# Weight sums mostly on GpSimd in a new order, the features' sum over tokens by fp32 column tiles, state products of two tiles together

## The chip, the cores and the metric

The kernel runs on one core of a Trainium2 chip. The metric is device time in microseconds (us) of one execution. A core has a matrix engine (PE; its weight loads are listed apart as PEld), three engines for elementwise work (DVE, the vector engine; ACT, the scalar engine; POOL, GpSimd), the queue engine SP that only starts DMAs, and DMA engines that move data between HBM and the on-chip memory SBUF. PSUM is the memory that the matrix engine writes to: eight banks of 128 x 512 fp32.

## The reference, cut to what matters

```python
S, D, H, Dh, F = 2048, 512, 32, 16, 1376
xn = layernorm(x)                                  # x: 2048 x 512
q, k, v = split_heads(xn @ wqkv)                   # 32 heads of 16
pq, pk = q @ w_phi, k @ w_phi                      # per head, 16 x 16
phi = concat(softmax(p), softmax(-p))              # for pq and pk: 32 features a head
kv = sum over tokens of phi_k^T v                  # per head 32 x 16
z  = sum over tokens of phi_k                      # per head 32
o  = (phi_q @ kv) / (phi_q . z + 1e-6)
s  = merge_heads(o) @ wo
h  = relu(xn @ W_gate) * (xn @ W_up)               # 2048 x 1376
out = x + s * silu(h @ W_down)
```

`z` is what the first line of the title calls the features' sum over tokens; `kv` is the state.

## The kernel before, in words

All products are done in a split form: a number is written as a high part (`h`) and a low part (`l`) that TensorE's fast fp32r mode takes, and `mm3` issues three matmuls (low x high, high x low, high x high) for each 128 rows of the inner dimension. Every instruction goes through a recorder (`InOrder`, line 60 of the profile), so all profile rows have the line L60 and are told apart by names.

**First part, tokens.** The 2048 tokens are 16 tiles of 128, `n` = 0..15. After two tiles by themselves, the loop `pair(m)`, m = 1..7, takes tiles n = 2m and n + 1 together. Each tile gets keys `pk`, values `pv`, queries `pq` (these go out to DRAM for later), the exponentials `ek` of the keys' features with their sums `sm` and reciprocals `rc`, and the product `ek * rc` = phi (`features_k`). `features_split` then starts a DMA from POOL's queue that adds phi to the buffer `zacc` (`zacc<-ek`; each waits in POOL's queue until the one before has landed, because both write `zacc`), and `kv_products` adds phi^T v of the tile to the PSUM bank `PKV`, in 16 small matmuls in four column tiles of 32.

From pair 3 on (`seven`, `FIRST = 3`) the key and value products of a pair use seven block products instead of eight. This needs sums of weight blocks, made once in pairs 1 to 3: `T[0]` to `T[3]`, each with two halves k = 0, 1 and a high and low part. The table `PLAN` says at which named point of which pair each step is issued, and on which engine: `vc20` is "on DVE (`v`), combine (`c`), sum 2, half 0"; `g` is POOL; `h` is the high part, always on ACT (`sh00`); `l` the low part. `T[0]` is needed first in pair 3 (the `pv` block), then `T[1]` and `T[2]` in the `pk` blocks, and `T[3]` (`th`) in the second half of the pair.

In pair 3 and later PE's order is: 6 matmuls `pk` (A11), 6 `pv` with `T[0]`, 6 `pk` with `T[1]`, 6 `pk` (A12), 6 `pk` with `T[2]`, [`kv_products(n - 2)`], transposes `pxT` of a coming tile, 12 `pq`, `kv_products(n - 1)`, 6 `pk` with `T[3]`, 6 `pv`, transposes, 12 `pq`. The same sums of columns are made of the tokens: POOL's `xf`, then `XT<-sb` and `XT<-xf`, which the `pv` block with `T[0]` of the next pair reads.

`MULT` names the engine of the product `ek * rc`: POOL for even tiles, DVE (None) for odd ones.

**Second part, the wide layer.** For f = 0..10 (128 of the 1376 columns, padded, each) `gate_up` does seven blocks of 6 matmuls (`pa`, `pb`, `pc`, `pd`), for each half of the tokens; `down` and `out_tile` follow (`py`, `pso`). In the first half `f_prep(f)` makes the weight sums of f: 6 copies on ACT, about ten operations on POOL (`tab`, `wa`, `wb`, `wc`, `wd`, `fdl`), and nine DMAs that spill the result to DRAM (`ws`), from which `f_reload` brings it back for the second half. f = 0 and 1 are prepared in pair 7, f in the block before it. At the same time `state()` turns the key state, and `q_pair` treats the saved queries; its GpSimd step `weigh` needs `zB`, the sum z.

**The sum z before.** When the last `zacc` DMA has landed, ACT copies the high part `zh`, POOL makes the low part `zl`, and four matmuls 128 x 512 (`pz`) with a matrix of ones sum over the partitions, which are tokens; ACT copies the diagonal pieces to `zB` in eight instructions. One matmul with `noughts` writes zeros to the upper half of `PKV` in pair 1.

**What sets the order.** `Clock` keeps a modelled time for each engine while the program is written. Background work is a list of generators; `pump()` advances each whose condition holds by the model. The order of each engine is fixed when the kernel is built. Nothing is reordered on the chip, apart from weight loads.

Of the kernel before, what the change touches and what calls it, by code (L numbers as in the profile page):

```python
# [10 lines left out]
ALU = mybir.AluOpType  # L11
# [21 lines left out]
UNITS = [*(((0, j), (1, j)) for j in range(2)), ((2, 0), (2, 1)),  # L33
         *(((q, j), (q + 1, j)) for q in (6, 4) for j in range(2)), ((3, 0), (3, 1))]
LAST = [2 * q + j for q in QUERIES[1] for j in range(2)][-3:]
AHEAD = ()
FIRST = 3
PLAN = {(1, "sums"): "vc50 vc51", (1, "split a"): "gc00", (1, "end"): "gc01", (2, "start"): "vc10", (2, "split b"): "vc11 vc20 gc21", (2, "scaled"): "gc30", (2, "mid"): "sh20 sh21 gl20 sh00 sh01 sh11", (2, "split a"): "vl11", (2, "turned"): "vl00 vl01 vc31", (2, "end"): "sh10 gl10 gc40", (3, "start"): "gl21 gc41 sh30", (3, "split b"): "gl30", (3, "sums"): "sh31", (3, "mid"): "vl31"}

START = (14, 15)  # L40
WO_WITH = (4, 5, 6, 7)
# [119 lines left out]
def layer_kernel(ctx: ExitStack, tc: tile.TileContext, x, wkT, wqT, wv, wo, wf, cst, out):  # L161
# [30 lines left out]
    def mm(o, w, m, start, stop):  # L192
        nc.tensor.matmul(o, w, m, start=start, stop=stop, skip_group_check=True)
# [288 lines left out]
    def kv_products(n):  # L482

        phi, v = PHI.pop(n).rearrange("p (j a c) s f -> p c j a (s f)", a=2, c=4), VH.pop(n)
        v = v.rearrange("p (c j x) -> p c j x", c=4, j=4)
        if n == 0:
            PKV.append(ps((P, 8, 64), name="pkv"))
        for j in range(4):
            for c in range(4):
                r = slice(32 * c, 32 * c + 32)  # L490
                nc.tensor.matmul(PKV[0][r, j], v[:, c, j], phi[:, c, j], start=n == 0 and j == 0,
                                 stop=n == N - 1, skip_group_check=True, tile_position=(0, 32 * c))
        if n == 0:
            mm(PKV[0].rearrange("p j x -> p (j x)")[:, 256:], noughts[:, :P], noughts, False, False)


    RAW, FT, WD = {}, {}, {}
# [7 lines left out]
    DONE = set()  # L505

    def f_load(f):
        if f in AHEAD[-1:]:

            t = u4((P, 2, 2, 2, P), "rawg")  # L510
            RAW[f] = [t[:, c] for c in range(2)], u2((P, D), "rawd")
            nc.sync.dma_start(t.rearrange("p c k s f -> p (c k s f)"), wf[f][:, :1024])
        else:
            RAW[f] = two("rawg", f not in AHEAD), u2((P, D), "rawd")
            for c in range(2):
                nc.sync.dma_start(RAW[f][0][c].rearrange("p k s f -> p (k s f)"), wf[f][:, c * 512:(c + 1) * 512])
        nc.sync.dma_start(RAW[f][1], wf[f][:, 1024:])

    def w_pair(name):
# [10 lines left out]
    def f_prep(f, keep=True):  # L530


        rg, rd = RAW.pop(f)
        b11, b12, b21, b22 = (rg[c][:, :, s, :] for c in range(2) for s in range(2))
        ta, tb = two("tab", keep)
        yield "gpsimd", b22
        add(nc.gpsimd, tb[:, 0], b12, b11, ALU.subtract)
        add(nc.gpsimd, ta[:, 1], b22, b12, ALU.subtract)
        wa = w_pair("wa")
        yield "scalar", b11  # L540
        for c in range(2):
            nc.scalar.activation(wa[0][:, c], rg[c][:, :, 0, :], AF.Copy)
        put(f, 0, wa[0])
        yield "gpsimd", ta
        add(nc.gpsimd, ta[:, 0], b22, tb[:, 0], ALU.subtract)
        add(nc.gpsimd, tb[:, 1], b21, ta[:, 0], ALU.subtract)
        wb = w_pair("wb")
# [24 lines left out]
        yield from sums_of(fd[1], rd, f32(fd[0]), ALU.subtract, fd[0])  # L572
        put(f, 8, fd[1])
        if keep:
            FT[f], WD[f] = [wa, wb, wc, wd], fd
            nxt = f + 1
            while nxt in AHEAD:
                nxt += 1
            del rg, rd, ta, tb
            if nxt < NF:  # L580
                f_load(nxt)
        DONE.add(f)
        yield None,
# [412 lines left out]
    noughts = u2((P, 256), "noughts", F32R)  # L996
    nc.vector.memset(f32(noughts), 0.0)
    zacc = u4((P, H, 2, DH), "zacc")

    WK, WV, WQ = w_tile("wk"), w_tile("wv"), w_tile("wq")  # L1000
# [115 lines left out]

    def all_preps():
        for f in AHEAD:
            f_load(f)
            yield 30,  # L1120
            yield from f_prep(f, False)
        while at[0] < START[0] - 1:
            yield 3,
        f_load(0)
        yield 30,
        for f in range(NF):
            if f not in AHEAD:
# [47 lines left out]
    def pair(m):  # L1175
# [48 lines left out]
        if news:  # L1224
            norm_scale(*news)
        t_steps(m, "scaled")
        kv_products(n - 2)
        pace.pump()
        at[0] = n + 1
        if n + 3 < N:  # L1230
# [46 lines left out]
        t_steps(m, "end")  # L1277
        pace.pump()

    EB, MULT = [], [nc.gpsimd, None]  # L1280
    for m in range(1, NP):
        pair(m)
    features_k(N - 1, *EB.pop())
# [2 lines left out]

    kvacc, zB = [None] * 2

    one, ones = u2((P, P), "one"), u2((P, P), "ones", F32R)
    nc.vector.memset(one, 1.0)  # L1290
    nc.scalar.activation(ones, one, AF.Copy)
    zhl = [u4((P, 1024), f"z{s}", F32R) for s in "hl"]
    kvt = sb.tile([P, NG, 32], F32, tag="kvt", bufs=1, name="kvt")
    nc.vector.memset(kvt, 0.0)
    q_load(0)
# [4 lines left out]
    def state():  # L1300
        nonlocal kvacc, zB
        kv_products(N - 1)

        kvacc = u2((P, 256), "kvacc")
        nc.scalar.activation(kvacc, PKV[0][:, :4].rearrange("p j x -> p (j x)"), AF.Copy)
        yield "vector", kvacc
        kvT = u2((P, 256), "kvT")
        nc.vector.transpose(kvT, kvacc)
        kvT = kvT.rearrange("p (j x f) -> p j x f", x=4, f=DH)
        kvacc = None  # L1310
        for c in range(4):
            r, h = slice(32 * c, 32 * c + 32), c % 2
            nc.vector.tensor_copy(kvt[r, :, DH * h:DH * h + DH].rearrange("p (j a) f -> p j a f", a=2), kvT[r, :, 0:4:3, :])
        zB = small(256, "zB", 1).rearrange("p (d x) -> p d x", d=4)
        while zhl[1].name not in pace.ready:
            yield 1,
        for a in range(2):
            yield "tensor", zhl[1]
            p = ps((P, 4, 4, 32), name="pz")
            for i, z in enumerate(zhl[::-1]):  # L1320
                mm(p.rearrange("p d i x -> p (d i x)"), ones, z[:, a * 512:(a + 1) * 512], i == 0, i == 1)
            for i in range(4):
                r = slice(32 * i, 32 * i + 32)
                nc.scalar.activation(zB[r, :, 32 * a:32 * a + 32], p[r, :, i, :], AF.Copy)

    def z_parts():
        yield "scalar", zacc
        nc.scalar.activation(zhl[0], flat(zacc), AF.Copy)
        yield "gpsimd", zhl[0]
        add(nc.gpsimd, zhl[1], flat(zacc), f32(zhl[0]), ALU.subtract)  # L1330
        yield None,

    def all_queries(half):
        if not half:
            pace.add(z_parts(), first=True)
# [161 lines left out]
```

## Time and profile before

| what | value |
|---|---|
| three runs | 564.0, 561.24, 562.82 us; median 562.82 us |
| the profiled execution's own time | 562.98 us |
| its span on the core | 561.2 us |
| PE busy | 548.0 us of the span (98%), 3149 matmuls |
| POOL busy | 347.9 us (62%) |
| DVE busy | 383.3 us (68%) |
| ACT busy | 263.6 us (47%) |
| mean granted TensorE clock | 0.991 |
| DMA moved | 125.45 MB, mean 224 GB/s |

The profiled execution took 562.98 us; 1.8 us of it lie around the span. How to read a row of a timeline: start in us, duration, engine, operation, output <- inputs, shapes, count; a bracket gives idle time of the engine before it and what ended it. Matmul rows overlap: in a full stream a 128 x 512 matmul starts every 0.227 us (six in 1.36 us), though each is shown with 0.39 us. fp32 matmuls count twice in the rows ("x32" for 16). "PEclk" is the clock that the chip granted TensorE, 1.00 for full speed.

### The profile page before, as it was taken

Reading aid. Unit: us, or ns where it says so; the run is one execution under the profiler, and the core shown is the slowest. Engines: PE = TensorE matmul, PEld = TensorE weight load, DVE = VectorE, ACT = ScalarE, POOL = GpSimd, SP = SyncE. Lnnn points to the kernel's source line nnn. Section 1 sums busy time; section 2 is a strip of 40 time slices with the busy share of each in tenths; the row PEclk is TensorE's granted clock in tenths of the full one; section 3 lists DMA queues with packets and bytes.
Section 4 is the critical chain, followed back from the end, with each engine's and each line's share of the span. In section 5 each row is a group of like instructions: output and inputs, shape, how many; then the busy total and the mean of one; then the engine's idle time right before and its main releaser. Section 6 shows DMA issues by size and latency. Waiting matters only on the chain.

```text
span 561.2 us, 9072 instructions
## 1 busy us (share of the span) xinstructions
PE 548.0 (98%) x3149; PEld 444.8 (79%) x3149; DVE 383.3 (68%) x588; ACT 263.6 (47%) x467; POOL 347.9 (62%) x309
## 2 busy tenths in 40 slices
PE   9999979999997999999999999999999999999997
PEld 8888758777775886887878888888778787878886
DVE  5998678867654669698953442599999496743323
ACT  3886656654542565646453142223564535342510
POOL 1566855542974999899996316352556584843491
PEclk9999979999999999999999999999999999999999
DMA  8359655646698767867697999594674462848063
GB/s 287 130 163 307 191 130 160 165 109 152 186 291 273 256 241 256 299 224 282 243 313 280 340 425 404 181 385 146 207 243 133 163 212 87 288 134 316 1 225 113
DMA packets 76223, 125.45 MB, mean 224 GB/s; under 512 B 6673, under 2 KB 29073, under 8 KB 75281
## 3 DMA queue, kind: packets, MB, share of 16 engines
q1 hardware_dynamic: 73872, 116.94, 59.7%
q0 software_dynamic: 2160, 7.87, 7.1%
q8 instruction: 25, 0.41, 0.3%
q14 instruction: 22, 0.17, 0.1%
q10 hardware_dynamic: 144, 0.07, 0.0%
HBM read 67.96 MB, written 48.50 MB: 208 GB/s over the span
## 4 chain that ended last, share of the span: by engine, by line
PE 77%; POOL 8%; DVE 5%; DMA 5%; issue 4%; ACT 0%; SPq 0%; POOLq 0%; DVEq 0%; ACTq 0%
PE py L60 18%; PE pk L60 9%; PE pd L60 8%; PE pa L60 8%; PE pso L60 8%; PE pq L60 7%; PE pb L60 7%; PE pc L60 4%; PE pv L60 4%; DMA zacc<-ek 2%; DMA wvr<-wv 2%; PE pkv L60 2%; POOL tab L60 1%; PE pnum L60 1%; POOL ez L60 1%
## 5 line engine op out<-in xcount | busy, mean ns | idle before, releaser
L60 PE MATMUL py<-fdh,hl 128*128 128x512 f32 x176 | 69.0, 392 | 0.0
L60 PE MATMUL py<-fdl,hh 128*128 128x512 f32 x176 | 68.5, 389 | 0.0
L60 PE MATMUL py<-fdh,hh 128*128 128x512 f32 x176 | 68.5, 389 | 0.0
L60 PE MATMUL pa<-XT,wa 128*128 128x512 f32 x264 | 67.3, 390 | 0.0
L60 PEld LDWEIGHTS pa<-XT,wa 128*128 128x128 f32 x264 | 49.4, 188 | 10.7 <-issue 0.4
L60 DVE TENSOR_TENSOR y<-py,y 128x512 f32<-128x512 f32 x40 | 27.5, 689 | 35.5 <-PE py L60 35.5
L60 POOL TENSOR_TENSOR hl<-t,hh 128x512 fp32r<-128x512 f32 x16 | 20.7, 1295 | 40.7 <-ACT hh L60 40.3
L60 POOL TENSOR_TENSOR y<-y,ys 128x512 f32<-128x512 f32 x24 | 30.9, 1292 | 17.4 <-ACT ys L60 17.1
L60 PE MATMUL pq<-XT,wqh 128*128 128x512 f32 (+1 forms) x144 | 40.5, 367 | 0.0
L60 PEld LDWEIGHTS py<-fdh,hl 128*128 128x128 f32 x176 | 33.0, 188 | 8.5 <-issue 1.2
L60 PEld LDWEIGHTS py<-fdh,hh 128*128 128x128 f32 x176 | 33.0, 188 | 6.9
L60 POOL TENSOR_TENSOR ez<-eq,zB 128x1024 f32<-128x1024 f32 x16 | 38.4, 2411 | 0.1
L60 PEld LDWEIGHTS py<-fdl,hh 128*128 128x128 f32 x176 | 33.0, 188 | 6.7
L60 ACT ACTIVATE hh<-t 128x512 fp32r<-128x512 f32 x16 | 10.1, 632 | 56.3 <-DVE t L60 53.0
L60 PE MATMUL pd<-XT,wd 128*128 128x512 f32 x132 | 34.2, 393 | 1.2 <-DVE t L60 1.2
L60 PE MATMUL pb<-XT,wb 128*128 128x512 f32 x132 | 34.3, 396 | 0.0
L60 PE MATMUL pd<-XT,wc 128*128 128x512 f32 x132 | 33.9, 391 | 0.0
L60 PE MATMUL pc<-XT,wb 128*128 128x512 f32 x132 | 33.5, 389 | 0.0
L60 DVE TENSOR_REDUCE mx<-pk 128x32 f32<-128x512 f32 x32 | 20.6, 684 | 18.8 <-PE pk L60 18.8
L60 POOL TENSOR_TENSOR ol<-of,oh 128x512 fp32r<-128x512 f32 (+1 forms) x13 | 19.8, 1550 | 20.3 <-ACT oh L60 20.3
L60 PE MATMUL pk<-wkh,XT 128*128 128x512 f32 x88 | 31.1, 405 | 0.0
L60 PEld LDWEIGHTS pd<-XT,wd 128*128 128x128 f32 x132 | 24.5, 188 | 7.7 <-POOL wd L60 1.6
(194 smaller groups left out, 1440.5 us busy)
## 6 DMA issues: line engine op xcount, KB each, us to landing
zacc<-ek POOLq DMA_DIRECT2D x15, 512.0 KB, 5.3
xts<-XT SPq DMA_DIRECT2D x4, 1792.0 KB
XT<-xts SPq DMA_DIRECT2D x7, 1024.0 KB, 6.7
rawg<-wf SPq DMA_DIRECT2D x22, 256.0 KB, 3.1
ws<-wa SPq DMA_DIRECT2D x22, 256.0 KB, 4.5
ws<-wb SPq DMA_DIRECT2D x22, 256.0 KB, 4.8
ws<-wc SPq DMA_DIRECT2D x22, 256.0 KB, 5.0
wa<-ws SPq DMA_DIRECT2D x22, 256.0 KB, 5.4
```

Source lines behind the costliest of these rows:

```text
L60: return self.tc.keep_in_program_order(op(*a, **k))
```

## The change

1. `PLAN`: most combine and low-part steps go to POOL (15 steps with `g`, 5 with `v`; before, 10 and 10), in a new order. The first ones come earlier in pairs 1 and 2.
2. `MULT`: both tiles' products `ek * rc` on POOL in the pair loop.
3. `kv_products(n - 2)` is issued right before `kv_products(n - 1)`, half a pair later than before.
4. z: the chain `zh`, `zl`, `pz` goes. Four fp32 matmuls with one column of 32 ones as weights, one for each column tile, read `zacc` itself and write to the upper half of `PKV`; one ACT copy makes `zB`. The `noughts` matmul goes.
5. `AHEAD`: f = 2 is loaded and prepared in pairs 4 to 6 (from tile 9 on), in large buffers, is spilled, and read back in the block of f = 1.

```diff
-AHEAD = ()
+AHEAD, AT = (2,), (9,)
 FIRST = 3
-PLAN = {(1, "sums"): "vc50 vc51", (1, "split a"): "gc00", (1, "end"): "gc01", (2, "start"): "vc10", (2, "split b"): "vc11 vc20 gc21", (2, "scaled"): "gc30", (2, "mid"): "sh20 sh21 gl20 sh00 sh01 sh11", (2, "split a"): "vl11", (2, "turned"): "vl00 vl01 vc31", (2, "end"): "sh10 gl10 gc40", (3, "start"): "gl21 gc41 sh30", (3, "split b"): "gl30", (3, "sums"): "sh31", (3, "mid"): "vl31"}
+PLAN = {(1, "sums"): "gc51", (1, "mid"): "gc50", (1, "split a"): "vc01 gc11", (1, "turned"): "gc00", (1, "end"): "gc10", (2, "start"): "vc21", (2, "sums"): "sh00 gc20", (2, "scaled"): "sh20 sh01 gl00", (2, "split a"): "sh21 gl20 gl01", (2, "turned"): "sh10 sh11 vc31 gl10", (2, "end"): "gl21", (3, "start"): "gc30 vl11 gc40 vc41", (3, "sums"): "sh30 sh31 gl30 gl31"}
...
-        if n == 0:
-            mm(PKV[0].rearrange("p j x -> p (j x)")[:, 256:], noughts[:, :P], noughts, False, False)
...
-        if f in AHEAD[-1:]:
-            t = u4((P, 2, 2, 2, P), "rawg")
-            RAW[f] = [t[:, c] for c in range(2)], u2((P, D), "rawd")
+        if f in AHEAD:
+            t = u8((P, 2, 2, 2, 2, P), "rawg")
+            RAW[f] = [t[:, 0, c] for c in range(2)], u2((P, D), "rawd"), [t[:, 1, c] for c in range(2)]
...
-        wa = w_pair("wa")
+        if keep:
+            wa, wb = w_pair("wa"), None
+        else:
+            t = u8((P, 4, 2, 2, P), "wab", F32R)
+            wa, wb = (t[:, 0], t[:, 1]), (t[:, 2], t[:, 3])
...
         for f in AHEAD:
+            while at[0] < AT[AHEAD.index(f)]:
+                yield 3,
             f_load(f)
             yield 30,
             yield from f_prep(f, False)
...
         t_steps(m, "scaled")
-        kv_products(n - 2)
         pace.pump()
...
         t_steps(m, "split a")
+        kv_products(n - 2)
         kv_products(n - 1)
...
-    EB, MULT = [], [nc.gpsimd, None]
+    EB, MULT = [], [nc.gpsimd, nc.gpsimd]
...
-    one, ones = u2((P, P), "one"), u2((P, P), "ones", F32R)
-    nc.vector.memset(one, 1.0)
-    nc.scalar.activation(ones, one, AF.Copy)
-    zhl = [u4((P, 1024), f"z{s}", F32R) for s in "hl"]
+    ones = small(32, "ones", 1)
+    nc.vector.memset(ones, 1.0)
...
+        yield "tensor", zacc
+        z = flat(zacc).rearrange("p (a d i x) -> p i a d x", a=2, d=4, i=4)
+        for i in range(4):
+            r = slice(32 * i, 32 * i + 32)
+            nc.tensor.matmul(PKV[0][r, 4:].rearrange("p (a b) (d x) -> p a (b d) x", a=2, x=32), ones, z[:, i], start=False,
+                             stop=True, skip_group_check=True, tile_position=(0, 32 * i))
         zB = small(256, "zB", 1).rearrange("p (d x) -> p d x", d=4)
-        while zhl[1].name not in pace.ready:
-            yield 1,
-        for a in range(2):
-            yield "tensor", zhl[1]
-            p = ps((P, 4, 4, 32), name="pz")
-            for i, z in enumerate(zhl[::-1]):
-                mm(p.rearrange("p d i x -> p (d i x)"), ones, z[:, a * 512:(a + 1) * 512], i == 0, i == 1)
-            for i in range(4):
-                r = slice(32 * i, 32 * i + 32)
-                nc.scalar.activation(zB[r, :, 32 * a:32 * a + 32], p[r, :, i, :], AF.Copy)
...
+        nc.scalar.activation(zB.rearrange("p d (a x) -> p a d x", a=2),
+                             PKV[0][:, 4:].rearrange("p (a b) (d x) -> p a (b d) x", a=2, x=32), AF.Copy)
```

**Place 1, POOL from the end of pair 2 into pair 3, before.** `l_854` and `l_855` are the low parts of `T[2]`, `l_865` that of the first half of `T[1]`, `t_815` and `t_816` lead to `T[3]`; the first `zacc` is that of tile 4.

```order
L60 TENSOR_TENSOR XT<-xf,XT 128x2x2x128
L60 DMA zacc<-ek 128x1024
L60 TENSOR_TENSOR l_865<-wvr,h_863 128x512
L60 TENSOR_TENSOR t_815<-t_815,wkl 128x512
L60 TENSOR_TENSOR l_855<-t_463,h_853 128x512
L60 TENSOR_TENSOR t_816<-t_816,wkl 128x512
L60 DMA zacc<-ek 128x1024
L60 TENSOR_TENSOR th<-t_815,th 128x512
```

The same place after the change: `l_818` and `l_819` are the low parts of `T[2]`, `l_810` that of the second half of `T[0]`, `l_953` that of the first half of `T[1]`, `t_957` leads to `T[3]`, and `ek` is the product of tile 5, which DVE did before.

```order
L60 TENSOR_TENSOR XT<-xf,XT 128x2x2x128
L60 DMA zacc<-ek 128x1024
L60 TENSOR_TENSOR l_818<-t_460,h_816 128x512
L60 TENSOR_TENSOR l_810<-wvr,h_809 128x512
L60 TENSOR_TENSOR l_953<-wvr,h_951 128x512
L60 TENSOR_TENSOR l_819<-t_461,h_817 128x512
L60 TENSOR_TENSOR ek<-ek,rc 128x1024
L60 TENSOR_TENSOR t_957<-wkh,wvr 128x512
L60 TENSOR_TENSOR t_957<-t_957,wkl 128x512
L60 DMA zacc<-ek 128x1024
```

Between the two `zacc` stand seven operations where there were four. Two of them, `l_810` and `l_953`, are read by PE in the first blocks of pair 3.

**Place 2, DVE at the same time, before:** `l_860` is the low part of `T[0]`.

```order
L60 TENSOR_TENSOR ek<-mx,pk 128x32x16
L60 TENSOR_TENSOR l_860<-wvr,h_859 128x512 x2
L60 TENSOR_TENSOR t_816<-wkh,wvr 128x512
L60 TENSOR_TENSOR XT<-pxT,XT 128x2x2x128
L60 TENSOR_REDUCE sm<-ek 128x64
L60 RECIPROCAL pk<-sm 128x64
L60 TENSOR_TENSOR ek<-ek,pk 128x1024
```

And after: `l_954` is the low part of the second half of `T[1]`; before the change it stood, as `l_866`, five instructions ahead of `l_860`.

```order
L60 TENSOR_TENSOR ek<-mx,pk 128x32x16
L60 TENSOR_TENSOR t_958<-wkh,wvr 128x512
L60 TENSOR_TENSOR XT<-pxT,XT 128x2x2x128
L60 TENSOR_REDUCE sm<-ek 128x64
L60 RECIPROCAL rc<-sm 128x64
L60 TENSOR_TENSOR l_954<-wvr,h_952 128x512
L60 TENSOR_TENSOR t_958<-t_958,wkl 128x512
```

The `T[0]` steps are gone from DVE; two steps with `t_958` and `l_954` stand there now, behind the sums of tile 5.

**Place 3, PE at the start of the second part, before,** from the state product of tile 15 to the matmuls of z:

```order
L60 MATMUL pkv<-ek,v 32x64 x16
L60 MATMUL pd<-XT,wc 128x512 x3
L60 MATMUL pc<-XT,wc 128x512 x6
L60 MATMUL pa<-XT,wa 128x512 x6
L60 MATMUL pd<-XT,wd 128x512 x6
L60 MATMUL pa<-XT,wa 128x512 x6
L60 MATMUL pz<-zl,ones 128x512
L60 MATMUL pz<-zh,ones 128x512
```

And after:

```order
L60 MATMUL pkv<-ek,v 32x64 x16
L60 MATMUL pd<-XT,wc 128x512 x3
L60 MATMUL pkv<-zacc,ones 32x256 x4
L60 MATMUL pc<-XT,wc 128x512 x6
L60 MATMUL pa<-XT,wa 128x512 x6
L60 MATMUL pd<-XT,wd 128x512 x6
L60 MATMUL pa<-XT,wa 128x512 x6
```

The matmuls of z stand 24 matmuls earlier in PE's order than before.

More of the change, by code (lines that the diff above doesn't have):

```diff
@@ L507, in f_load @@
     def f_load(f):
-        if f in AHEAD[-1:]:
-            t = u4((P, 2, 2, 2, P), "rawg")
-            RAW[f] = [t[:, c] for c in range(2)], u2((P, D), "rawd")
-            nc.sync.dma_start(t.rearrange("p c k s f -> p (c k s f)"), wf[f][:, :1024])
-        else:
-            RAW[f] = two("rawg", f not in AHEAD), u2((P, D), "rawd")
-            for c in range(2):
-                nc.sync.dma_start(RAW[f][0][c].rearrange("p k s f -> p (k s f)"), wf[f][:, c * 512:(c + 1) * 512])
+        if f in AHEAD:
+            t = u8((P, 2, 2, 2, 2, P), "rawg")
+            RAW[f] = [t[:, 0, c] for c in range(2)], u2((P, D), "rawd"), [t[:, 1, c] for c in range(2)]
+        else:
+            RAW[f] = two("rawg", True), u2((P, D), "rawd"), None
+        for c in range(2):
+            nc.sync.dma_start(RAW[f][0][c].rearrange("p k s f -> p (k s f)"), wf[f][:, c * 512:(c + 1) * 512])
         nc.sync.dma_start(RAW[f][1], wf[f][:, 1024:])
@@ L530, in f_prep @@
     def f_prep(f, keep=True):
-        rg, rd = RAW.pop(f)
+        rg, rd, tab = RAW.pop(f)
         b11, b12, b21, b22 = (rg[c][:, :, s, :] for c in range(2) for s in range(2))
-        ta, tb = two("tab", keep)
+        ta, tb = tab or two("tab", True)
         yield "gpsimd", b22
@@ L546, in f_prep @@
         add(nc.gpsimd, tb[:, 1], b21, ta[:, 0], ALU.subtract)
-        wb = w_pair("wb")
+        wb = wb or w_pair("wb")
         yield "scalar", ta
@@ L578, in f_prep @@
                 nxt += 1
-            del rg, rd, ta, tb
+            del rg, rd, ta, tb, tab
             if nxt < NF:
@@ L995, in layer_kernel @@
     nc.vector.memset(mhalf, -0.5)
-    noughts = u2((P, 256), "noughts", F32R)
-    nc.vector.memset(f32(noughts), 0.0)
     zacc = u4((P, H, 2, DH), "zacc")
@@ L1313, in state @@
             nc.vector.tensor_copy(kvt[r, :, DH * h:DH * h + DH].rearrange("p (j a) f -> p j a f", a=2), kvT[r, :, 0:4:3, :])
-        zB = small(256, "zB", 1).rearrange("p (d x) -> p d x", d=4)
-        while zhl[1].name not in pace.ready:
-            yield 1,
-        for a in range(2):
-            yield "tensor", zhl[1]
-            p = ps((P, 4, 4, 32), name="pz")
-            for i, z in enumerate(zhl[::-1]):
-                mm(p.rearrange("p d i x -> p (d i x)"), ones, z[:, a * 512:(a + 1) * 512], i == 0, i == 1)
-            for i in range(4):
-                r = slice(32 * i, 32 * i + 32)
-                nc.scalar.activation(zB[r, :, 32 * a:32 * a + 32], p[r, :, i, :], AF.Copy)
[L1326 to L1331, printed above, removed]
+        yield "tensor", zacc
[4 more added lines that the diff above has]
+                             stop=True, skip_group_check=True, tile_position=(0, 32 * i))
+        zB = small(256, "zB", 1).rearrange("p (d x) -> p d x", d=4)
+        nc.scalar.activation(zB.rearrange("p d (a x) -> p a d x", a=2),
+                             PKV[0][:, 4:].rearrange("p (a b) (d x) -> p a (b d) x", a=2, x=32), AF.Copy)
     def all_queries(half):
         if not half:
-            pace.add(z_parts(), first=True)
             yield from state()
```

## The prediction, made before the changed kernel had run

> **What bounds the kernel now.** I read the page's busy times first, then the waits of PE, then PE's timeline where it waits.
>
> ```profile
> PE 548.0 (98%) x3149; PEld 444.8 (79%) x3149; DVE 383.3 (68%) x588; ACT 263.6 (47%) x467; POOL 347.9 (62%) x309
> ...
> PE pz L60 <- POOL zl L60: 3.4, 1, 3.4
> PE pv L60 <- DVE l L60: 2.5, 1, 2.5
> PE pd L60 <- DVE t L60: 1.2, 1, 1.2
> ...
> PE pk L60 <- ACT pk L60: 1.0, 1, 1.0
> ...
> 70.00:84.00 14.00, 10.40 (x62) 7.36 (x62) 11.00 (x18) 6.85 (x14) 7.10 (x6) 0.76 0.56 134
> ```
>
> PE sets the time: 548.0 of 561.2 us busy. Work taken from another engine is worth something only where PE waits for it, and that is in few places. The two large ones are the places that the change touches. The window from 70 to 84 us (the column after POOL's is the granted clock) shows that a wait costs more than itself: at a mean clock of 0.76, 14 us lose 3.4 us of full speed.
>
> The first hole is the start of pair 3:
>
> ```profile
> 68.46 0.39 PE L60 MATMUL pk<-wkh,XT 128*128 128x512 f32 x1
> ...
> 72.74 0.47 PE L60 MATMUL pv<-l,XT 128*128 128x512 f32 x1 [2.53 <-DVE l L60]
> ...
> 75.12 0.79 PE L60 MATMUL pk<-h,XT 128*128 128x512 f32 x1 [0.98 <-ACT pk L60]
> ...
> 82.68 0.65 PE L60 MATMUL pkv<-ek,v 128*32 128x64 f32 x32
> ```
>
> Between 68.46 and 82.68 stand 30 matmuls, which in a full stream take 30 x 0.227 = 6.8 us. They took 14.2, so this hole costs **7.4 us**: idle time, and then half clock. The second hole is the sum z:
>
> ```profile
> 171.59 1.53 PE L60 MATMUL pc<-XT,wc 128*128 128x512 f32 x6
> ...
> 175.68 1.52 PE L60 MATMUL pa<-XT,wa 128*128 128x512 f32 x6
> 180.63 0.80 PE L60 MATMUL pz<-zl,ones 128*128 128x512 f32 x1 [3.43 <-POOL zl L60]
> ...
> 184.58 1.54 PE L60 MATMUL pc<-XT,wb 128*128 128x512 f32 x6
> ```
>
> After `pa` (175.68 + 1.36 = 177.04; six matmuls take 6 x 0.227 = 1.36) only the 6 matmuls of `pb` would stand before 184.58 without z: 178.4. This hole costs **6.2 us**, `pz` itself included.
>
> **Change 1, the sums' steps.** What makes DVE late before is in POOL's and DVE's timelines around 65 us, and, for a second case, near 212 us (the two short rows are from the chain of waits):
>
> ```profile
> 57.92 0.87 POOL L60 DMA_DIRECT2D zacc<-ek  x1 [5.73 <-DVE XT L60]
> 58.53 1.59 POOL L60 TENSOR_TENSOR wvr<-wvr 128x512 f32<-128x512 f32 x1
> 59.79 1.00 POOL L60 TENSOR_TENSOR lr<-lr,mhalf 128x2 f32<-128x2 f32 x1
> ...
> 61.74 1.69 POOL L60 TENSOR_TENSOR xf<-xf,sb 128x256 f32<-128x256 f32 x2
> ...
> 64.38 2.17 POOL L60 TENSOR_TENSOR ek<-ek,rc 128x1024 f32<-128x1024 f32 x1
> 66.28 1.53 POOL L60 TENSOR_TENSOR XT<-sb,XT 128x512 fp32r<-128x512 f32 x1
> 67.52 1.53 POOL L60 TENSOR_TENSOR XT<-xf,XT 128x512 fp32r<-128x512 f32 x1
> ...
> 64.70 4.91 DVE L60 TENSOR_TENSOR l<-wvr,h 128x512 fp32r<-128x512 f32 x1 [3.54 <-POOL l L60]
> ...
> 74.33 1.20 DVE L60 TENSOR_REDUCE sm<-ek 128x64 f32<-128x1024 f32 x1
> 75.56 0.56 DVE L60 RECIPROCAL pk<-sm 128x64 f32<-128x64 f32 x1
> ...
> 211.84 1.80 DVE L60 SCALAR_TENSOR_TENSOR qd<-qs 128x64 f32<-128x64 f32 x1
> ...
> 211.61 1.25 POOL hl L60
> 212.86 0.70 POOL tab L60
> ```
>
> The DVE operation at 64.70, with both inputs in SBUF, took 4.91 us. It ended at 69.61, some 0.6 us after POOL's run of `ek`, `XT`, `XT` (to 69.05). So it did not get in at POOL's boundaries at 66.3 and 67.5. The small one at 211.84 sat through `hl` and `tab` in the same way and ended at 213.64, just after POOL's 213.56, where POOL's next operation had to wait for its own predecessor. My reading: such a DVE operation waits until POOL has a gap.
>
> The Trainium skill says (SBUF — State Buffer, "Who interferes with whom") that a DVE instruction with two SBUF inputs contends with a GpSimd one that reads SBUF, and that the second to issue is blocked until the first finishes. The trace agrees on the contention; the 4.91 us span three POOL instructions, where the page speaks of one. By the page's rule the first rival below would come true.
>
> Now the walk with the new order. Before the change `zacc` of tile 3 starts at 57.92; I keep that. Spacings come from the starts above: 1.25 for 512 columns, 0.7 `lr`, 1.4 `xf`, 1.9 `ek`, 0.6 to 0.7 for issuing a DMA. POOL then does one combine (59.8), `lr` (60.5), `l` of `T[0]`'s first half (61.7), `xf` (63.1), `ek` (65.0), two `XT` (67.5), `zacc` of tile 4 (68.2), and without a gap `l_818` (69.4), `l_810` (70.7), `l_953` (71.9), `l_819` (73.2), `ek` of tile 5 (75.1), `t_957` (76.3). The next `t_957` depends on it: a gap. DVE comes to `t_958`, two SBUF inputs, after its `ek` pieces, near 65, and gets in during the `zacc` issue, to 68.2. Then `XT` 0.6, `sm` 1.2, `rc` 0.55: it asks for `l_954` at 70.6, inside POOL's run, and finishes it at **77.0**.
>
> PE reaches pair 3 about 0.6 us earlier than before (change 2), so its `T[0]` block starts at 69.2. It needs the second half's `l_810` at 70.1: 0.6 late. It needs `l_953` at 71.4: 0.5 late. It needs `l_954` at 72.8: 4.2 late. That is 5.3 us idle, and after such an idle time I put the same loss of clock as before, 3.4 us: 8.7 against 7.4. **+1.3 us** (bounds: -0.4 where half the clock loss is spared, +3 where DVE gets in only behind the `zacc` of tile 5). The moved steps themselves, some five of 1.25 us from DVE to POOL, cost nothing else: no later wait of PE names them.
>
> Both `ek` on POOL (14 us more, 7 x 1.9) and f = 2's preparation (ten operations, about 9.6 us by the ones of f = 0) lie in pairs 3 to 7. They must not delay the sums for the next pair's `pv`:
>
> ```profile
> 119.59 0.57 POOL L60 TENSOR_TENSOR lr<-lr,mhalf 128x1 f32<-128x1 f32 x1 [3.17 <-DVE lr L60]
> ...
> 126.00 1.30 POOL L60 TENSOR_TENSOR XT<-xf,XT 128x512 fp32r<-128x512 f32 x1
> ...
> 129.71 1.36 PE pv L60 x6
> ```
>
> In pair 5 `XT` ends at 127.3, 2.4 us before `pv`. Of the new work only `wc` (1.3) falls between `xf` and `XT`, and 0.6 of ACT's new copies ahead of `vb`; the rest falls where POOL idles (3.17 here). 0.5 us is left: cost 0. Where that cover fails, each us late is a us of PE.
>
> **Change 2, state products together.**
>
> ```profile
> 54.85 0.39 PE L60 MATMUL pv<-wvh,XT 128*128 128x512 f32 x1
> 55.17 0.65 PE L60 MATMUL pkv<-ek,v 128*32 128x64 f32 x32
> ...
> 65.02 0.40 PE L60 MATMUL pv<-wvh,XT 128*128 128x512 f32 x1
> 65.26 0.60 PE L60 MATMUL pxT<-ident,xt 128*128 128x128 f32 x4
> ```
>
> With 16 products between, `pxT` starts at 55.75 (the row after 55.17), 0.90 after the last `pv`; without, 0.24. One group alone costs 0.66. Behind another group it costs at most its own 0.58 (55.17 to 55.75), and at least 0.45 if its turn-around goes too. That saves 0.08 to 0.21 in each of 7 pairs, plus 0.2 for the `noughts` matmul: 0.8 to 1.7, I take **-1.1**. Phi of the odd tile now comes from POOL; it is needed half a pair later, after 12 `pq`.
>
> **Change 3, the sum z.** PE comes to z 24 matmuls earlier. Its input is the landed `zacc`:
>
> ```profile
> 161.08 0.88 POOL L60 DMA_DIRECT2D zacc<-ek  x1 [2.56 <-DMA zacc<-ek]
> ...
> 166.94 10.07 DMA zacc<-ek
> ...
> 177.10 1.06 ACT L60 ACTIVATE zh<-zacc 128x1024 fp32r<-128x1024 f32 x1 [5.79 <-DMA zacc<-ek]
> ...
> DMA to landing us min/median/max: 2.9/5.2/10.1
> ```
>
> The last DMA landed at 177.0, and PE stands at z at 171.6. It waits 5.4 us, does four matmuls of 256 columns (as many columns as one state group, 0.58; twice that at half clock: 1.1), and then runs at half clock for some 4 us, as it did from 180.63 to 184.58, which loses 1.8. That is 8.3 against 6.2: **+2.1**. The chain `zh`, `zl` and nine ACT copies saved do not help, since PE now waits for the DMA itself. With a landing in 5.2 us the wait would be 0.5 and the step worth -5.0; I take the row of this very DMA, since the same spills and loads of f = 0 and 1 run beside it. What z feeds (`weigh`) comes some tens of us later.
>
> **Change 5, the wide layer.** POOL is freed of f = 2's work; PE waits there once, 1.2 us for `t`. Bounds -1.2 to 0; I take 0, since that wait hangs on DVE's queue. Nine reads of 256 KB come into the block of f = 1, ahead of their use.
>
> **Sum.** 1.3 - 1.1 + 2.1 + 0 = +2.3 on the profiled 562.98 us (0.16 above the median): **565.3 us**.
>
> **Rival 1: DVE gets in between POOL's instructions.** Then `l_954` follows `l_810`: 71.3, in time for 72.8. Pair 3 loses 1.1 instead of 7.4, and no clock: -6.3 - 1.1 + 2.1 = -5.3, **557.7 us**. For it: the step's new place leaves DVE only three operations before. Against it: both rows above. If z lands early as well, 553.
>
> **Rival 2: the chain of `zacc` comes late, slower.** In pair 7 POOL has two `ek` (3.8 us) more before the last DMAs, each of which waits for the one before; the wait of 2.56 at 161.08 is all the room. In the new order `wb` and `wc` (2.5) go behind, which should pay for it. If they don't, because the first `ek` waits for DVE, all three DMAs are 3.8 us late and PE waits that much longer at z: **569 us**. It decides once POOL issues tile 13's `zacc` later, against PE, than before.
>
> **How the numbers follow.** Forecast 0.40 (own range 561 to 568), rival 1 0.35, rival 2 0.25. About 0.5%, 2.8 us, is what can be told from no change: 560.0 to 565.6. Faster: nearly all of rival 1 and a bit of the forecast's early landing, 0.35. Slower: rival 2 and nearly half of the forecast, 0.40. Same: 0.25. The range takes in rival 1 and rival 2: 555 to 570.
>
> **What would show it.** In the changed profile: a DVE `l` of 5 us or more near 71 and PE's `pk` waiting for it (forecast) or one under 2 us (rival 1); PE `pkv<-zacc` waiting for the DMA for about 5 us; no `pv` that waits for `XT` in pairs 4 to 7. A `zacc` landing before PE gets to z, or a POOL gap in pair 3 that I don't see, would make the forecast wrong.

## The result, and the profile after

The changed kernel takes 562.81 us (median of 20 runs, 560.46 to 564.71); the kernel before, on the same chip, 562.78 us. The ratio is 0.9997, 95% interval 0.9982 to 1.0012: no difference, where +2.3 us (0.4%) was forecast. The profiled execution has a span of 561.7 us (before 561.2), a granted clock of 0.988 (0.991), PE busy 545.8 us, DVE 381.4, ACT 259.3 and POOL 364.4 (16.5 more than before).

The waits of PE in the changed kernel (engine and place, what was waited for, sum in us, times, longest):

```profile
PE pkv L60 <- DMA zacc<-ek: 5.0, 1, 5.0
PE pk L60 <- DVE l L60: 3.7, 1, 3.7
PE pv L60 <- POOL l L60: 1.1, 1, 1.1
...
PE pc L60 <- DVE e L60: 0.4, 1, 0.4
PE pd L60 <- DVE t L60: 0.3, 1, 0.3
```

The two holes are where the prediction put them, with the causes it named: z waits for the landing of `zacc`, and the start of pair 3 waits for `l` of DVE. The old waits for `zl` (3.4) and for DVE's `l` in `pv` (2.5) are gone, and the one for `t` has shrunk from 1.2 to 0.3.

DVE and POOL before and in pair 3, from the changed kernel's timelines:

```profile
62.46 2.16 POOL L60 TENSOR_TENSOR ek<-ek,rc 128x1024 f32<-128x1024 f32 x1
...
66.85 1.13 POOL L60 DMA_DIRECT2D zacc<-ek  x1
67.48 1.82 POOL L60 TENSOR_TENSOR l<-t,h 128x512 fp32r<-128x512 f32 x1
68.73 3.03 POOL L60 TENSOR_TENSOR l<-wvr,h 128x512 fp32r<-128x512 f32 x2
71.22 1.78 POOL L60 TENSOR_TENSOR l<-t,h 128x512 fp32r<-128x512 f32 x1
75.95 2.25 POOL L60 TENSOR_TENSOR ek<-ek,rc 128x1024 f32<-128x1024 f32 x1 [2.95 <-DVE rc L60]
...
63.76 9.79 DVE L60 TENSOR_TENSOR t<-wkh,wvr 128x512 f32<-128x512 f32 x1
...
75.79 0.63 DVE L60 TENSOR_TENSOR l<-wvr,h 128x512 fp32r<-128x512 f32 x1
```

The held operation is `t_958`, two inputs in SBUF, 9.79 us. It ends 0.55 us after POOL's run of `l` ends (71.22 + 1.78 = 73.0) and POOL itself has to wait for `rc`. So it passed seven of POOL's boundaries (a boundary is where one POOL instruction ends and the next follows), the issue of the `zacc` DMA among them, where my walk had let it in. `l_954`, which PE waits for, is only late behind it: it asks at 75.8 instead of 70.6, takes 0.63 us and is done at 76.4 (forecast: held itself, done at 77.0). POOL's own `ek` then starts late too, because its `rc` stands in the same queue behind `t_958`.

PE there (start, duration):

```profile
67.10 0.39 PE L60 MATMUL pk<-wkh,XT 128*128 128x512 f32 x1
...
76.47 0.80 PE L60 MATMUL pk<-l,XT 128*128 128x512 f32 x1 [3.69 <-DVE l L60]
...
82.08 0.60 PE L60 MATMUL pxT<-ident,xt 128*128 128x128 f32 x4
```

30 matmuls worth 6.8 us take 82.08 - 67.10 = 14.98: the hole is 8.2 us, against 7.4 before; the granted clock from 70 to 84 us is 0.76, as before. And z, with the window around it (the granted clock is the column after POOL's):

```profile
168.67 0.96 PE L60 MATMUL pd<-XT,wc 128*128 128x512 f32 x3
174.67 1.08 PE L60 MATMUL pkv<-zacc,ones 128*32 128x256 f32 x8 [5.04 <-DMA zacc<-ek]
175.68 2.93 PE L60 MATMUL pc<-XT,wc 128*128 128x512 f32 x6
178.41 2.47 PE L60 MATMUL pa<-XT,wa 128*128 128x512 f32 x6
...
184.84 1.52 PE L60 MATMUL pc<-XT,wb 128*128 128x512 f32 x6
188.13 1.65 PE L60 MATMUL pc<-XT,wc 128*128 128x512 f32 x6 [0.41 <-DVE e L60]
...
168.00:182.00 14.00, 8.96 (x62) 6.25 (x62) 5.11 (x9) 1.40 (x3) 5.65 (x6) 0.76 1.03 343
```

From the end of `pd` (168.67 + 0.8) to `pc` at 184.84 stand z and five blocks of 1.36 us: 15.4 - 6.8 = 8.6 us for z. The same stretch before, 171.59 to 184.58, is the 6.2 of the prediction. `pc` and `pa` take 2.93 and 2.47 where 1.5 is usual: half clock, and a mean of 0.76 over the window.

How far PE is ahead of the kernel before (start of the same matmul, after minus before), and so where each part of the change shows:

| place | before | after | difference | what came in between |
|---|---|---|---|---|
| first `pk` of pair 1 | 30.36 | 29.75 | -0.61 | 0.25 us wait for `wvl` before, and what went with it |
| first `pk` of pair 3 | 68.46 | 67.10 | -1.36 | products together in pairs 1 and 2, no `noughts` |
| first `pk` of pair 4 | 93.25 | 92.45 | -0.80 | hole +0.8, products together |
| first `pk` of pair 7 | 145.16 | 143.50 | -1.66 | products together, three times |
| `pa` of f = 0 | 165.22 | 163.11 | -2.11 | pair 7 |
| `pc` after z | 187.32 | 188.13 | +0.81 | z +2.4, wait for `e` and the restart behind it +0.5 |
| `pnum` | 220.81 | 220.86 | +0.05 | wait for `t` 1.2 to 0.3 |

The gain of products together runs through all seven pairs and is given back in two places. From `pnum` on PE keeps step (its last matmul starts 0.13 us later); the rest of the 0.5 us between the two spans lies behind it.

### The profile page after: what moved, and what is told of

It is laid out like the page before. It is cut to its first block, busy times and chain, and to the rows that moved or that the text cites. A ratio compares the mean times of both kernels' runs of the same rounds, so it can differ in the third digit from the quotient of the medians.

```text
span 561.7 us, 9081 instructions
## 1 busy us (share of the span) xinstructions
PE 545.8 (97%) x3152; PEld 444.5 (79%) x3152; DVE 381.4 (68%) x576; ACT 259.3 (46%) x458; POOL 364.4 (65%) x319
## 4 chain that ended last, share of the span: by engine, by line
PE 83%; DVE 9%; DMA 2%; issue 2%; POOL 2%; ACT 1%; SPq 1%; DVEq 0%; POOLq 0%; ACTq 0%
PE py L60 19%; PE pk L60 9%; PE pd L60 8%; PE pa L60 8%; PE pso L60 8%; PE pq L60 7%; PE pb L60 7%; PE pc L60 5%; PE pv L60 5%; DVE t L60 2%; DMA zacc<-ek 2%; PE pkv L60 1%; PE pfold L60 1%; PE pnum L60 1%; POOL ez L60 1%
## 5 line engine op out<-in xcount | busy, mean ns | idle before, releaser
L60 POOL TENSOR_TENSOR hl<-e,hh 128x512 fp32r<-128x512 f32 x6 | 7.7, 1291 | 35.0 <-ACT hh L60 26.9
```

The lines of the kernel that those rows point to most:

```text
L60: return self.tc.keep_in_program_order(op(*a, **k))
```

## The experiments

All ratios are to the kernel before, with the 95% interval. Where a part is changed, the base is the changed kernel unless it is said otherwise. "By the middles" compares two ratios and leaves their intervals out.

**`z_late`: z 12 matmuls later.** How much of the loss at z follows from its place?

```diff
         yield "tensor", zacc
+        yield 12,
```

> The changed kernel with z put 12 matmuls later in PE's order, behind pc and pa of the wide layer; nothing else is changed. Theory: z costs 8.6 us in the changed kernel because PE stands there (5.0 us for the landing of zacc, then half clock). Behind 12 more matmuls of 0.227 us (2.7 us) PE still waits about 2.3 us, so the wait falls by 2.7 us and about 1 us of the half clock with it: 562.8 - 3 to 4 = about 559. Rival: the landing moves along with PE (the DMA is late because of what PE and its neighbours do), then the wait stays at 5 us and the time at 562.8. Second rival: the whole loss goes, 555, if the wait of 2.3 us costs no clock.

Measured: 556.75 us, ratio 0.9913 (0.9881 to 0.9945), span 557.6 (4.1 less than the changed kernel's). The wait for `zacc` is 2.7 us (the theory had 2.3): the landing does not move along. z costs 5.2 us in this trace in place of 8.6, and the wait for `e` is gone: together -3.8, within the interval. The median is lower than the 559 of the theory, between it and the 555 of the second rival: the traced execution, 559.42 us, is the slowest of the five (see the last section).

**`psum1`: the held DVE step, one step freed.** ACT copies the input `wvr` of `t_958` to PSUM; the DVE step has then one input in SBUF.

```diff
-                    add(engine, by_parity(o), by_parity(f32(wh)), raw[k + 2], ALU.subtract)
+                    p = ps(name="pt")
+                    nc.scalar.activation(p, wv_raw[:, k + 2, :], AF.Copy)
+                    add(engine, by_parity(o), by_parity(f32(wh)), even_first(p), ALU.subtract)
```

> The changed kernel, but DVE's first step of t_958 gets its wvr from PSUM, where ACT copies it first; that step then has one input in SBUF. Theory (a DVE operation with two SBUF inputs is held until GpSimd has a gap): t_958 takes 0.7 instead of 9.8 us and starts near 68.8, XT, sm and rc follow by 71.8, and now l_954, still with two SBUF inputs, is the one that is held: GpSimd has rc early, so it runs on with ek and t, and l_954 takes 4 to 5 us and ends near 76.7. PE waits for it as before, 3 to 4 us: 562.8, within 1.5. Rival (DVE gets in between two GpSimd instructions, and t_958 was held by something of its own): l_954 takes under 2 us, PE waits under 1 us, 557.

Measured: 563.12 us, ratio 1.0015 (1.0000 to 1.0031). DVE and POOL of this kernel:

```profile
68.89 0.69 DVE L60 TENSOR_TENSOR t<-wkh,pt 128x512 f32<-128x512 f32 x1 [4.88 <-ACT pt L60]
...
71.81 4.93 DVE L60 TENSOR_TENSOR l<-wvr,h 128x512 fp32r<-128x512 f32 x1
...
72.55 2.42 POOL L60 TENSOR_TENSOR ek<-ek,rc 128x1024 f32<-128x1024 f32 x1
74.44 1.74 POOL L60 TENSOR_TENSOR t<-wkh,wvr 128x512 f32<-128x512 f32 x1
76.26 1.61 POOL L60 TENSOR_TENSOR t<-t,wkl 128x512 f32<-128x512 f32 x1
```

The same step takes 0.69 us, and the hold-up moves to the next DVE step with two inputs in SBUF: `l_954` asks at 71.8, is held for 4.93 us past the boundaries at 72.5 and 74.4, and gets in near 76.1, where POOL's `t` depends on the `t` before it. PE waits 3.9 us for it (3.7 in the changed kernel). This is the walk of the prediction itself, one step later than in the changed kernel.

**`psum2`: all three steps freed.** In addition `l_954` reads PSUM, and `t_958` lies in PSUM between its two steps.

```diff
+                    add(engine, even_first(p), by_parity(f32(wh)), even_first(p), ALU.subtract)
+                elif k in PT:
+                    add(engine, by_parity(o), even_first(PT.pop(k)), by_parity(f32(wl)))
...
+            if i == 1 and engine.key == "vector":
+                p = ps(name="pl")
+                nc.scalar.activation(p, wv_raw[:, k + 2, :], AF.Copy)
+                src = even_first(p)
```

> As psum1, and in addition l_954 gets its wvr from PSUM and t_958 lies in PSUM between its two steps, so none of the three DVE steps in this stretch has two SBUF inputs. Theory: all three take 0.6 to 0.8 us, l_954 is done at about 72.4, PE waits at most 0.3 us for it, and of the 8.2 us that the start of pair 3 loses some 2 are left: about 557. Rival 1: the hole moves on, PE then waits 2 us or more for the th of GpSimd in the next block: 560. Rival 2: the place of the inputs is not what holds DVE; a step still takes over 3 us and the time stays at 562.8.

Measured: 557.93 us, ratio 0.9920 (0.9890 to 0.9951). DVE's two steps, and PE at the end of the stretch:

```profile
72.27 0.63 DVE L60 TENSOR_TENSOR l<-pl,h 128x512 fp32r<-128x512 f32 x1
72.82 0.68 DVE L60 TENSOR_TENSOR t<-pt,wkl 128x512 f32<-128x512 f32 x1
...
67.04 0.39 PE L60 MATMUL pk<-wkh,XT 128*128 128x512 f32 x1
...
76.40 0.60 PE L60 MATMUL pxT<-ident,xt 128*128 128x128 f32 x4
```

The hole is 76.40 - 67.04 - 6.8 = 2.6 us, with a granted clock of 1.00 from 70 to 84 us; 1.4 of it is PE's wait for POOL's `l`. Rivals 1 (a new wait for `th`) and 2 of this run's expectation are out. The place of the inputs is what held DVE.

**`psum2_z` and `psum2_z24`: both holes, and z later still.**

> psum2 and z_late together. If both theories hold and the two holes are independent, the gains add: 562.8 - 6 - 3.5 = about 553.5. If PE, being earlier, only waits longer for the landing of zacc (the landing hangs on GpSimd's and the DMA queue's pace, not on PE's), the 6 us of the first part come back as wait at z: about 559.

Measured: 553.49 us, ratio 0.9846 (0.9807 to 0.9885). PE still waits 2.8 us at z. So:

```diff
-        yield 12,
+        yield 24,
```

> psum2_z with z 24 matmuls later than the changed kernel has it, not 12. In psum2_z PE still waits 2.8 us at z; another 12 matmuls are 2.7 us. Theory: the wait is all but gone, 553.5 - 2.8 = 550.7. Rival: what z feeds, or the bank that it holds, now comes late and PE waits for it some blocks later: 553.5.

Measured: 550.44 us, ratio 0.9800 (0.9781 to 0.9820), which is 11.4 us under the 561.88 us of the kernel before in these runs. The waits of PE that are left, beside 1.1 us at the very start, are 1.2 for POOL's `l`, 1.1 for DVE's `t`, 0.5 for `xt` and one of 0.3. z now costs 0.8 us. This kernel computes the whole reference and beats both. The wait for `t` is back at 1.1.

**`z24`: z 24 matmuls later alone** (`yield 24,` in the changed kernel).

> The changed kernel with z 24 matmuls later, nothing else changed (the new table of steps with its held DVE step stays). Theory: the wait and the half clock at z go altogether, 8.6 us less 0.6 for z's own matmuls and 0.9 for the wait for t that the two kernels with z in that place show again: 562.8 - 7 = 555.5 to 556. Rival: the two holes are not independent, and most of what psum2_z24 gained came from the earlier start: 559.

Measured: 556.09 us, ratio 0.9882 (0.9850 to 0.9915); the wait for `zacc` is 0.3, the one for `t` 1.1. With `psum2` alone at 0.9920 the product is 0.9803, and both together gave 0.9800: the two holes are independent, within these intervals.

**`warm`: is it the idle time or the clock at z?** 20 matmuls fill the wait.

```diff
         yield "tensor", zacc
+        p = ps(name="pwarm")
+        for _ in range(20):
+            mm(p, XT[:, A11, 0, 0, :P], XT[:, A11, 0, 0, :], True, True)
```

> The changed kernel with 20 matmuls of 512 columns put ahead of z, into a bank that nobody reads: they add work whose result is not used. They take 4.5 us of the 5.0 us that PE waits there. Theory: the wait for zacc stays in time but PE no longer idles, so it does not fall to half clock: z's matmuls take 0.6 instead of 1.0, and pc, pa behind it 1.5 each instead of 2.9 and 2.5: 562.8 - 2.7 = 560.1. Rival: the clock follows something other than PE's idle time, the matmuls behind z stay slow: 562.8; if the landing moves back under more PE traffic, 564.

Measured: 560.81 us, ratio 0.9976 (0.9957 to 0.9996). PE around z:

```profile
169.62 4.71 PE L60 MATMUL pwarm<-XT 128*128 128x512 f32 x20
174.26 0.64 PE L60 MATMUL pkv<-zacc,ones 128*32 128x256 f32 x8
174.83 1.66 PE L60 MATMUL pc<-XT,wc 128*128 128x512 f32 x6
...
168.00:182.00 14.00, 14.00 (x97) 10.83 (x96) 6.35 (x14) 2.52 (x5) 4.38 (x5) 1.00 1.06 357
```

z takes 0.64 instead of 1.08 and `pc` 1.66 instead of 2.93. PE runs on at full clock (1.00 in the window, 0.76 without the 20 matmuls), and z and the `pc` behind it take 1.7 us less than in the changed kernel, 2.6 with the `pa` behind that. So in these traces the half clock follows PE's idle time. In the total, the middles of the two ratios lie 1.2 us apart and the intervals overlap: the sign of the theory, its 2.7 us not reached for certain.

**`merge_alone`: the state products together, alone,** on the kernel before (`kv_products(n - 2)` moved as in the change; `noughts` stays).

> The kernel before, with one part of the change alone: the state products of two tiles together, in 7 pairs (the noughts matmul stays). By the prediction's price this saves 0.08 to 0.21 us a pair: 0.6 to 1.5 us in all, 561.3 to 562.2. By what the changed kernel's trace shows (pair period 17.18 us against 17.47) it saves 0.29 a pair, 2.0 us: 560.8. Rival: the shorter pair period comes from the moved ek of GpSimd or from something else in the pair, then this kernel stays at 562.8, or above if phi of the odd tile is still in DVE's hands and comes late.

Measured: 560.25 us, ratio 0.9982 (0.9965 to 0.9999): -1.0 us, -2.0 to 0. Its trace has the pair period of the changed kernel: `pxT` at 105.25 and 122.43, 17.18 us apart, against 107.51 and 124.98, 17.47 apart, before. So the 0.29 us a pair come from this part alone. Over seven pairs that is 2.0 us, the far end of the interval; the total by itself can't tell it from the 1.1 of the prediction.

**`old_z`: the old sum z** in the changed kernel (`zh`, `zl`, four `pz`, 24 matmuls later).

> The changed kernel with the sum z as it was before (zh on ACT, zl on GpSimd, four pz matmuls of 512 columns, 24 matmuls later). Theory: the fp32 column tiles in their new place cost 2.4 us more than the old sum (8.6 against 6.2): 562.8 - 2.4 = 560.4, with PE waiting about 3 us for zl. Rival: the time of z hangs on when zacc lands alone and the two forms cost the same: 562.8.

Measured: 560.04 us, ratio 0.9984 (0.9961 to 1.0006). The interval holds both the changed kernel's 0.9997 and a gain of 2 us; it doesn't settle the size (by the middles the old sum is 0.7 us better). PE waited 3.9 us for `zl` and 1.1 for `t`.

**`old_plan`: the old table of steps** in the changed kernel (the `PLAN` of before).

> The changed kernel with the old table of steps (which sums' step runs on DVE or GpSimd, and when). Theory: the start of pair 3 loses 8.2 us in the changed kernel and 7.4 before, so the new table is worth +0.8: 562.0, and DVE's l before pair 3 is again the one that is held for some 5 us. Rival: with both ek on GpSimd the old table fits worse and the hole grows, 565 or more (the new table is then what the moved ek needed).

Measured: 561.88 us, ratio 0.9995 (0.9979 to 1.0011), the same as the changed kernel. DVE's `l` at 62.21 is held for 6.41 us and PE waits 3.1 for it; the hole is 8.0 us. The new table moved the hole from `l` to `t_958`; in time no gain or loss can be told here (the old table is 0.1 us better by the middles).

**`phi_dve`: phi of the odd tile on DVE again.**

```diff
-    EB, MULT = [], [nc.gpsimd, nc.gpsimd]
+    EB, MULT = [], [nc.gpsimd, None]
```

> The changed kernel with phi of the odd tile on DVE again, as before the change. The prediction put its move to GpSimd at nothing. If it is nothing, 562.8. Theory from the changed trace: at the start of pair 3 this multiplication stands ahead of l_954 in DVE's queue, 1.2 us, and the pairs have slack elsewhere: 564.

Measured: 570.0 us, ratio 1.0126 (1.0098 to 1.0155), far over both expectations. DVE at the start of pair 3, PE and ACT in pair 5:

```profile
64.36 10.92 DVE L60 TENSOR_TENSOR t<-wkh,wvr 128x512 f32<-128x512 f32 x1
...
77.63 1.22 DVE L60 TENSOR_TENSOR ek<-ek,pk 128x1024 f32<-128x1024 f32 x1
...
125.82 1.65 PE L60 MATMUL pk<-th,XT 128*128 128x512 f32 x6 [1.97 <-ACT vb L60]
...
125.17 0.60 ACT L60 ACTIVATE vb<-pk 128x512 f32<-128x512 f32 x1 [4.82 <-POOL fdl L60]
```

Two things I had not seen. POOL no longer has an `ek` that waits for `rc`, so the gap that let `t_958` in at 73.0 is gone; it is held to 75.3. Then phi stands ahead of `l_954` (which starts at 78.77), and PE waits 6.2 us: the hole is 10.6 us in place of 8.2. And the program's order changes elsewhere, because the background work is placed by the modelled load of the engines: f = 2's preparation comes where ACT's `vb` has to wait for POOL's `fdl`, 2.0 us of PE, and a `pv` waits 0.9 for `XT`. That is 5 us of the 7; the rest I did not trace to single waits.

**`no_ahead`: f = 2 not prepared ahead** (`AHEAD, AT = (), ()`).

> The changed kernel without preparing f = 2 ahead; its weights are prepared in their turn as before. The prediction put this part at nothing (-1.2 to 0). If it is nothing, 562.8; PE then waits 0.3 us for t as in the changed kernel, because that wait follows z's place. Rival: it was this part that took 0.9 us of the wait for t away, 563.7, with PE waiting 1.2 us for t.

Measured: 561.8 us, ratio 0.9987 (0.9967 to 1.0007). PE waits 0.3 us for `t`, as in the changed kernel. So this part did not shorten that wait, and its worth can't be told from nothing, as forecast (by the middles the kernel without it is 0.6 us faster).

## Why the prediction missed, step by step

The forecast was +2.3 us; what was measured is 0.0, with an interval of -1.0 to +0.7. The mechanisms were right at both holes; the sum was wrong in its sizes. As far as the traces tell, two terms failed, each by more than 1 us: z at +2.1, taken from one row, where the traces together show about +0.6; and the state products at -1.1, where PE's starts show -2.2.

**Change 2, the state products: a term of half the size.** The prediction took -1.1 in all, 0.08 to 0.21 a pair; the trace shows 0.29 a pair, 2.0 for seven and 0.2 for `noughts`, 2.2 in all. Here is the count, PE of the kernel before, then of the changed one:

```profile
99.82 0.39 PE L60 MATMUL pk<-h,XT 128*128 128x512 f32 x1
...
100.73 0.66 PE L60 MATMUL pxT<-ident,xt 128*128 128x128 f32 x4
101.14 0.48 PE L60 MATMUL pq<-XT,wql 128*128 128x512 f32 x1
...
104.07 0.65 PE L60 MATMUL pkv<-ek,v 128*32 128x64 f32 x32
104.65 1.65 PE L60 MATMUL pk<-th,XT 128*128 128x512 f32 x6
```

```profile
99.02 0.39 PE L60 MATMUL pk<-h,XT 128*128 128x512 f32 x1
99.25 0.60 PE L60 MATMUL pxT<-ident,xt 128*128 128x128 f32 x4
99.61 0.48 PE L60 MATMUL pq<-XT,wql 128*128 128x512 f32 x1
...
102.54 1.10 PE L60 MATMUL pkv<-ek,v 128*32 128x64 f32 x64
103.57 0.73 PE L60 MATMUL pk<-th,XT 128*128 128x512 f32 x2
```

A group by itself costs (101.14 - 99.82) - (99.61 - 99.02) = 0.73 us, not 0.66: the transposes behind it hand over 0.05 later too, and the prediction stopped its count at the start of `pxT`. Behind another group it costs 1.03 - 0.58 = 0.45, the low end of the prediction's 0.45 to 0.58, of which it took the middle: the whole turn-around goes. 0.73 - 0.45 = 0.28 a pair. This size rests on the traces; the total of `merge_alone`, -1.0 (-2.0 to 0), holds both the forecast's and this one.

**Change 1, the sums' steps: right in kind, near in size.** +1.3 forecast, +0.8 in the profiled execution, where PE idled 5.0 us for the forecast's 5.3. In the six traces with nothing changed at this place (the changed kernel, `z_late`, `z24`, `warm`, `no_ahead`, `old_z`) the hole is 7.4 to 9.2 us, 8.2 in the mean; in the three with the old table it is 6.4 (`merge_alone`), 7.4 (before) and 8.0 (`old_plan`), 7.3 in the mean. That two inputs in SBUF are what holds the DVE operation beside POOL is shown by `psum1` and `psum2`: with one input in PSUM the same step takes 0.69 instead of 9.79 us, and the hold-up goes to the next step that still has two. The victim was misnamed by one step, since I let `t_958` in at the issue of the `zacc` DMA. By SBUF — State Buffer of the Trainium skill, "Who interferes with whom", such a DVE instruction contends with GpSimd's reads, one with at most one SBUF input (outside the 2-port modes) does not, and the one that loses is blocked. The first two agree with these runs (9.79 against 0.69 us). The length does not follow from one blocking instruction: 9.79 us span eight POOL instructions, one of them the DMA issue. That it waits for a gap of POOL holds in these rows, but not everywhere (last section). Rival 1, that DVE gets in between them, is out at this place.

**Both `ek` on POOL at cost 0:** no `pv` waits for `XT` in pairs 4 to 7, as forecast. But it is not a part by itself: with the new table and phi on DVE the kernel takes 570.0. Some 2.4 of these 7 us are the hole at pair 3, which grows to 10.6. So the table needs the move, and the prediction priced the two apart.

**Change 3, z: right mechanism, a size that one trace can't carry.** +2.1 forecast, +2.4 in the profiled execution, by the same wait and the same half clock. That the two lie so near is partly luck, since z costs a different amount from trace to trace. Counted as above, it is 8.6, 6.9 (`psum1`), 6.2 (`psum2`), 5.9 (`old_plan`), 6.5 (`no_ahead`) and 9.0 us (`phi_dve`) in the six kernels with z in its new place, 7.2 in the mean, with waits of 3.6 to 5.9 us; and 6.2 (before), 6.5 (`merge_alone`) and 7.2 (`old_z`; 7.7 with its next block, which still runs slow) in the three with the old form, 6.6 to 6.8 in the mean. The difference is nearer to +0.6 than to +2.4, and `old_z` points the same way (0.7 by the middles). The prediction had the low side in its bounds (-5.0 at a landing of 5.2 us) and took the one row. Its rival 2 is out: the last two `zacc` DMAs were issued at 157.97 and 165.79, earlier than the 161.08 and 166.94 of before, and the last landed at 174.5, not at 177.0.

**The wide layer: 0 forecast, -0.8 + 0.5 seen.** The wait for `t` is 1.1 or 1.2 us in all five kernels with z 24 matmuls later (before, `merge_alone`, `old_z`, `z24`, `psum2_z24`) and 0.2 or 0.3 in all with z earlier, f = 2 ahead or not. It belongs to z's place. So does the wait of 0.4 for `e`: the kernels with z ahead of `pc` have it, `z_late` and `z24` do not. The prediction looked for it in POOL's load and left it out of z's term.

**What stays open.** With these sizes (pair 3 +0.8, products -2.2, z +0.6, its neighbours -0.3) the sum is -1.1 us, about the lower end of the interval, -1.0. By the middles of the runs with one part changed (products -1.0, z +0.7, table +0.1, f = 2 ahead +0.6) it is +0.4, but each of these can be off by 1 us or more. So it is not settled how the miss divides between z and the products. Executions of one kernel also differ: those of the changed kernel at a granted clock of 0.994 took 560.5 and 560.6 us, those at 0.988 563.1 to 564.1, and the profiled one, 563.54, is 0.7 above the median. The -0.6 before pair 1 is none of the change: the 0.25 us wait for `wvl` is also in `old_z` and `warm`, and not in the others.

**Two slips that the forecast does not use.** 7 x 1.9 is 13.3, not 14 us of `ek`. And rival 1 with an early landing comes by its own terms (-6.3 - 1.1 - 5.0) to 550.6, not 553.

## What to carry to other kernels

Where a DVE step with two inputs in SBUF stands beside a busy GpSimd and PE waits for it, it can be freed by giving it one operand from PSUM, when a third engine has time to put it there: three steps, two copies on ACT and 5 us here. When several steps of one queue are exposed, freeing one only moves the hold-up to the next, so free them all before judging. A consumer of a late DMA belongs as far back in PE's order as its own consumers allow; here 24 matmuls were worth 6.5 us.

## What the runs showed of the hardware

**Equal waits, unequal clocks.** PE waited 2.74 us at z in `z_late` and 2.79 in `psum2_z`, after the same two blocks, and then, first in `z_late`:

```profile
175.18 0.64 PE L60 MATMUL pkv<-zacc,ones 128*32 128x256 f32 x8 [2.74 <-DMA zacc<-ek]
175.75 2.19 PE L60 MATMUL pd<-XT,wd 128*128 128x512 f32 x6
177.73 2.62 PE L60 MATMUL pa<-XT,wa 128*128 128x512 f32 x6
```

```profile
170.34 0.64 PE L60 MATMUL pkv<-zacc,ones 128*32 128x256 f32 x8 [2.79 <-DMA zacc<-ek]
170.91 1.65 PE L60 MATMUL pd<-XT,wd 128*128 128x512 f32 x6
```

The two blocks behind took 4.4 us in the one (to `pb` at 180.19) and 2.9 in the other (to `pb` at 173.78), at full clock 2.7; the granted clock from 168 to 182 us is 0.88 and 1.00. The five executions of `z_late` differ in the same way: three took 556.1 to 556.8 us at 0.997, two 559.0 and 559.4 at 0.989 and 0.994. TensorE: Matmul & The Clock Gate of the Trainium skill (Part 1) has the gate watch PE's activity in windows of some 3.4 us that run freely, so that the moment of a change depends on where in a window the work lands. The two rows agree with that, and no run here shows the windows themselves.

**DVE does get in at a boundary, twice.** In the changed kernel:

```profile
43.49 1.54 DVE L60 TENSOR_TENSOR wvr<-wvr,wkh 128x512 f32<-128x512 f32 x1
...
43.17 1.31 POOL L60 TENSOR_TENSOR t<-wvr 128x512 f32<-128x512 f32 x1
44.43 2.39 POOL L60 TENSOR_TENSOR ek<-ek,rc 128x1024 f32<-128x1024 f32 x1
...
76.33 2.42 DVE L60 TENSOR_TENSOR t<-t,wkl 128x512 f32<-128x512 f32 x1
...
78.17 1.73 POOL L60 TENSOR_TENSOR t<-wkh,wvr 128x512 f32<-128x512 f32 x1
```

In the first case DVE asks at 43.5 and is done at 45.0, so it got in near the end of POOL's `t` at 44.4, and POOL's `ek` took 2.39 us, 0.5 longer than the 1.9 from start to start elsewhere. In the second, the step behind `l_954` asks at 76.3, is done at 78.75, and so got in where POOL's `ek` ends (75.95 + 2.25 = 78.20); POOL's `t` then ends 1.7 us behind `ek`, for an operation of 1.25. In neither case did POOL have to wait for an operation of its own. What sets these boundaries apart from the seven that `t_958` passed wasn't tried. One thing differs in the rows: here POOL's next instruction starts 0.03 to 0.05 us before the one ahead of it ends, at the boundaries that `t_958` passed 0.26 to 0.57 us. It doesn't decide alone, since the small operation at 211.84 in the kernel before passed a boundary with 0.05.
